# Taking the end-of-chunk decays from L itself, and moving small work off TensorE, in a Mamba-2 scan followed by an ELU feed-forward

## The chip, the cores and the metric

The kernel runs on one core of a Trainium2 chip. The metric is the device time of one execution in microseconds. Engines are called as in the profile: PE is TensorE (PEld its weight loads), DVE is VectorE, ACT is ScalarE, POOL is GpSimd, SP is the engine that issues nearly all DMAs.

## What is computed

Two stages, cut from the reference:

```python
# stage 1: x (4, 8, 768, 32), a (4, 8, 768), B and C (4, 8, 768, 16), chunk 32 there
cum = np.cumsum(log(a) of the chunk)
L = np.exp(cum[i] - cum[j]) * (i >= j)
y = (C B^T * L) x  +  (C state) * exp(cum)
state = exp(cum[last]) * state + sum_j B_j x_j exp(cum[last] - cum[j])
# stage 2: the y of all heads side by side, (3072, 256); w_in (256, 2048), w_out (2048, 256)
h = y @ w_in
g = np.where(h > 0, h, np.exp(np.minimum(h, 0)) - 1)
out = g @ w_out
```

The factor exp(cum[last] - cum[j]) is what the change is about: it is also the last column (i = last) of L.

## The kernel before, in words

**Blocks.** The 3072 tokens are cut into twelve blocks of 256 tokens, n = 0 to 11. A block is one batch entry's 256 tokens with all eight heads. The code's chunk is Q = 64 tokens, so a block has four chunks: halves u of 128 tokens, each with two chunks v. In words of the change, "block three" is n = 2 and "block four" is n = 3.

**Stage 1 of a block.** `load_bc(n)` and `load_x(n)` load B, C and x. `spread_cum(n)` loads the running sums, spread over partitions, into the tile L (partition j, then head, half u, column i). `decay_of(n, h)` turns L in place into exp(cum[i] - cum[j]) for one head, two ACT instructions of line 481, and after every fourth head POOL masks four heads in two instructions (L486). `turn(n)` transposes B and C by four PE transposes into PSUM (L389); ACT copies B to `bct` (L393) and DVE makes `ctm`, C masked by heads (L396). For n > 3 the loads come in another layout ("squares") and DVE transposes them instead: `turn_part(n, 0)` turns C, `turn_part(n, 1)` turns B (L413), `turn_part(n, 2)` makes `ctm` from SBUF (L421), `turn_part(n, 3)` makes `cts`, C times exp(cum) (L404). `first_exp(n)` makes exp(cum) spread over state rows, the tile `ec`, by a matmul with 0/1 weights `heads` (L368) and an ACT copy (L372), for n < 3; `spread_exp(n)` loads it from DRAM (`flat_exp`) for n > 2. `scaled(n)` (L379, POOL) makes `sc`, B times exp(cum[last] - cum[j]); that factor comes from the table `eb`, which `rest_of_sums` and one `turned(E, "eb", ...)` make once for n > 1. `scores(n)` are 16 small matmuls C B^T (L501, tile `g`); `weigh(n, q)` multiplies a quarter of them by L (L510, tile M); `sums(n)` are 16 small matmuls of `sc` and x (L531, tile `st`); `states(n)` chains four states S_new on DVE (L548) with a masked copy Sx on POOL (L553); `across(n)` and `inside(...)` are the matmuls that make y (L576, L595), and the copies of y to `yT` (L612).

**Stage 2.** `l1(n, i)` makes one eighth of h of block n in one PSUM bank (L627, 128x256 matmuls; with parts=2 each is cut into two of 128 columns). `elu()` takes the oldest entry of `lag`: ACT relu and exp (L640, L647), DVE combines (L649) to `g`. `l2(n, j)` multiplies `g` by two row blocks of w_out (L748). From n = 4 on a pair of blocks goes through a seven-product scheme (L699 in `front`, `mid`, `back`; L809 in `second`).

**Weights.** They arrive as 64-bit words in 16 pieces and are made into 32-bit ones on the chip: `w_take(i)` is ACT Abs (L174), a DVE low word (L183) and DVE sign (L192); `w_give(i)` is DVE L200 and L207 and then a POOL addition (L217). Pieces 8 to 15 are w_out; `l2(n, j)` needs piece 8 + j. Piece 8 is made in step 7 of the loop described next, 9 in step 9, and 10 to 15 in steps 0 to 5 of the loop of n = 2.

**Order.** The schedule is written out by hand: each engine runs its instructions in program order. After a start in which blocks 0 and 1 are brought up, a loop over twelve steps s runs the l1 of blocks 0 and 1, each step followed by pieces of block 2's stage 1. Then a loop over n = 2, 3 and i = 0 to 7 runs `l2(n - 2, i)`, `l1(n, i)`, with the stage 1 of blocks 3, 4 and 5 in `scan_ahead` and beside it; then pairs of blocks in 16 steps k each. [...] a pool of seven, `p_a`, whose buffers are given out again in the order in which they came free, and one in `p_o`.

**End.** `second(n)` sums the output of the last two blocks in the tile `c_sum`, whose parts are (block, half, column half). `store(n, at)` writes one block, 256 KB.

## Time and profile before

| | us |
|---|---|
| median of three runs (lowest, highest) | 359.23 (358.4, 359.25) |
| the profiled execution | 357.64 |
| its span in the trace | 355.9 |
| PE busy, PEld busy | 349.0, 313.4 |
| DVE, ACT, POOL busy | 242.5, 200.5, 231.8 |
| last DVE add ends | 352.5 |

The span runs from the first to the last record of the trace; the device time has 1.7 us more around it. The busy times are sums of instruction durations, so they say nothing of where in the span an engine is full; the page's 40 slices (8.9 us each) do. The profiled execution is 1.6 us below the median of the runs, so differences worked out in it are added to the median. The mean TensorE clock was 0.998 of full speed.

### The profile page before, as it was taken

To read this page: it belongs to the slowest core of one execution; us is meant where nothing else is said; L and a number is where in the kernel's file an instruction comes from. 1 tells how busy PE (TensorE), PEld (TensorE's weight loads), DVE (VectorE), ACT (ScalarE), POOL (GpSimd) and SP (SyncE) were. 2 spreads that over 40 slices of the span, in tenths; PEclk is the share of its full clock that TensorE was granted. 3 is DMA by queue.
4 is the path that set the end of the run, shared out by engine and by line. 5 is a ranking of instruction groups with operands and counts; after the bars stand their busy time and mean duration, and the time that the engine had idled before them with its cause. 6 is when DMAs were issued, how large, how long until landed. Compare 5 with 4: busy or idle time off the path is not lost.

```text
span 355.9 us, 9943 instructions
## 1 busy us (share of the span) xinstructions
PE 349.0 (98%) x3962; PEld 313.4 (88%) x3962; DVE 242.5 (68%) x500; ACT 200.5 (56%) x491; POOL 231.8 (65%) x367
## 2 busy tenths in 40 slices
PE   8899999999999999999999999999999999999995
PEld 5579888888888999899999899999899999999995
DVE  3999987993999768674677684677674555656212
ACT  4759969867425577535577535576635544444000
POOL 5553643663676997869477769477769444464973
PEclk9999999999999999999999999999999999999999
DMA  8978998470460500146500145600000100000001
GB/s 156 209 195 155 246 318 174 96 122 31 72 139 2 120 0 3 19 98 132 113 0 2 17 102 112 133 3 0 2 2 4 59 3 0 2 0 33 29 2 60
DMA packets 82742, 26.36 MB, mean 74 GB/s; under 512 B 59720, under 2 KB 78600, under 8 KB 82696
## 3 DMA queue, kind: packets, MB, share of 16 engines
q1 hardware_dynamic: 80520, 25.53, 32.2%
q8 instruction: 31, 0.51, 0.6%
q10 hardware_dynamic: 2176, 0.20, 0.5%
q14 instruction: 15, 0.12, 0.1%
HBM read 22.38 MB, written 3.34 MB: 72 GB/s over the span
## 4 chain that ended last, share of the span: by engine, by line
PE 93%; DVE 3%; ACT 1%; POOL 1%; issue 0%; POOLq 0%; DVEq 0%
PE ps_o L809 35%; PE ps_h L699 28%; PE ps_h L627 14%; PE ps_o L748 8%; PE ps_y L595 2%; PE ps_g L501 2%; PE ps_y L576 1%; PE ps_st L531 1%; PE ps_idle L232 1%; DVE mag L207 1%; DVE mag L200 1%; DVE M L510 1%; DVE sgn L192 0%; DVE g L649 0%; POOL w_in L217 0%; ACT L L471 0%
## 5 line engine op out<-in xcount | busy, mean ns | idle before, releaser
L640 ACT ACTIVATE e<-ps_h 128x512 f32<-128x512 f32 x96 | 57.0, 593 | 89.5 <-DVE ps_h L724 44.0
L809 PEld LDWEIGHTS ps_o<-w_out,g 128*128 128x128 f32 x640 | 79.9, 192 | 3.1 <-issue 0.5
L809 PE MATMUL ps_o<-w_out,g 128*128 128x128 f32 x640 | 81.0, 275 | 0.0
L649 DVE SCALAR_TENSOR_TENSOR g<-e,ps_h 128x512 f32<-128x512 f32 x96 | 65.1, 679 | 10.5 <-ACT e L647 10.4
L627 PE MATMUL ps_h<-yT,w_in 128*128 128x256 f32 (+1 forms) x272 | 60.9, 371 | 1.7 <-POOL w_in L217 1.7
L647 ACT ACTIVATE e<-e 128x512 f32<-128x512 f32 x96 | 60.9, 635 | 2.0
L776 POOL TENSOR_TENSOR g<-g 128x256 f32<-128x256 f32 x33 | 23.9, 726 | 54.4 <-DVE g L649 54.4
L627 PEld LDWEIGHTS ps_h<-yT,w_in 128*128 128x128 f32 x272 | 48.4, 190 | 9.5 <-POOL w_in L217 3.1
L809 PE MATMUL ps_o<-w_sum,g 128*128 128x128 f32 x320 | 42.9, 275 | 0.0
L809 PEld LDWEIGHTS ps_o<-w_sum,g 128*128 128x128 f32 x320 | 41.1, 192 | 1.2
L481 ACT ACTIVATE L<-L,ncum 128x64 f32<-128x64 f32 x160 | 41.0, 337 | 0.0
L699 PE MATMUL ps_h<-yT,w_in 128*128 128x256 f32 x128 | 38.8, 385 | 0.0
L732 DVE TENSOR_TENSOR ps_h<-ps_h,u_sum 128x512 f32<-128x512 f32 x32 | 22.3, 698 | 23.5 <-PE ps_h L699 23.4
L699 PE MATMUL ps_h<-y_sum,w_in 128*128 128x256 f32 x128 | 38.1, 380 | 0.0
L699 PE MATMUL ps_h<-y_sum,w_sum 128*128 128x256 f32 x128 | 38.1, 380 | 0.0
L486 POOL TENSOR_SCALAR_AFFINE_SELECT L<-L 64x512 f32<-64x512 f32 x40 | 28.8, 719 | 10.8 <-ACT L L481 9.5
L716 DVE TENSOR_TENSOR u_sum<-ps_h,u_sum 128x512 f32<-128x512 f32 x32 | 22.1, 689 | 14.5 <-ACT u_sum L709 8.1
L724 DVE TENSOR_TENSOR ps_h<-ps_h,u_sum 128x256 f32<-128x256 f32 x32 | 13.8, 432 | 26.3 <-PE ps_h L699 26.3
L748 PE MATMUL ps_o<-w_out,g 128*128 128x256 f32 x128 | 30.8, 384 | 0.0
L764 POOL TENSOR_TENSOR t<-g 128x256 f32<-128x256 f32 x40 | 28.9, 756 | 0.3
L764 POOL TENSOR_TENSOR g<-g,t 128x256 f32<-128x256 f32 x40 | 28.8, 752 | 0.3
L764 POOL TENSOR_TENSOR g<-t,g 128x256 f32<-128x256 f32 x40 | 27.9, 730 | 1.1 <-PE ps_o L809 1.1
(111 smaller groups left out, 533.9 us busy)
## 6 DMA issues: line engine op xcount, KB each, us to landing
L<-flat SPq DMA_DIRECT2D x20, 256.0 KB
w<-in_moe_w_in_dram SPq DMA_DIRECT2D x8, 512.0 KB
w<-in_moe_w_out_dram SPq DMA_DIRECT2D x8, 512.0 KB
xr<-in_x_dram SPq DMA_DIRECT2D x24, 128.0 KB
out_dram<-c_sum SPq DMA_DIRECT2D x10, 256.0 KB
bc<-in_B_dram SPq DMA_DIRECT2D x24, 64.0 KB
bc<-in_C_dram SPq DMA_DIRECT2D x22, 64.0 KB
ec<-flat_exp SPq DMA_DIRECT2D x9, 128.0 KB
```

What stands on the lines that cost most here:

```text
L481: nc.scalar.activation(L[:, h, u], L[:, h, u], ACT.Exp, bias=ncum[:, u, row:row + 1])
L486: nc.gpsimd.affine_select(out=part, in_=part, pattern=[[0, 4], [0, 2], [1, Q]], compare_op=ALU.is_ge, fill=0.0, base=0, channel_multiplier=-1)
L627: nc.tensor.matmul(out=ps[:, j, toks], lhsT=w_in[:, k, m * P:(m + 1) * P], rhs=yT[n // 2][:, k, n % 2].rearrange("p u i -> p (u i)")[:, toks],
L640: nc.scalar.activation(begun[0], lag[0][2], ACT.Relu, scale=-1.0)
L647: nc.scalar.activation(e, e, ACT.Exp, scale=-1.0)
L649: nc.vector.scalar_tensor_tensor(out=g_of[n, i], in0=e, scalar=1.0, in1=ps, op0=ALU.subtract, op1=ALU.max)
L699: nc.tensor.matmul(out=out, lhsT=lhsT, rhs=rhs, start=first, stop=True, skip_group_check=True)
L732: nc.vector.tensor_tensor(out=c2, in0=c2, in1=u[:, 0:2], op=ALU.add)
L748: nc.tensor.matmul(out=o_of[n][:, ts], lhsT=g_of[n, j][:, m % 2, ts * P:(ts + 1) * P], rhs=w_out[:, m], start=(m == 0 and ts == 0), stop=( ...
L764: nc.gpsimd.tensor_tensor(out=out, in0=in0, in1=in1, op=ALU.subtract)
L776: eng.tensor_tensor(out=b12, in0=b12, in1=b11, op=ALU.subtract)
L809: nc.tensor.matmul(out=ps[:, ts], lhsT=b[:, ts * P:(ts + 1) * P], rhs=a[:, i], start=(i == chunk[0] and ts == 0), stop=(i == chunk[-1]), s ...
```

## The change

1. **No table of decays.** `rest_of_sums`, the table `eb` (one POOL subtraction, one ACT exp, two PE transposes, one DVE copy) go. `scaled(n)` for n > 1 takes its factor from the last column of L after the masks, so it now follows all eight `decay_of`. For n = 2 it moves from step 4 to step 7; for n = 5 from i = 0 to i = 1. For n >= 6 the decays start one pair of steps earlier.
2. **exp(cum) of n = 2 by a load.** `spread_exp(2)` on SP, after `spread_cum(2)`, in place of `first_exp(2)`; the third `heads` goes.
3. **n = 3 turned by VectorE.** `load_bc(3)` brings the squares and the extra copy `b_tok`; `turn_part(3, 0..3)` at i = 0 to 3 replace `turn(3)` and `turn_exp(3)` at i = 1.
4. **Bursts joined.** `scores(2)` moves from step 7 to step 8, directly ahead of `sums(2)`; the `weigh`s of n = 2 and the y products move with it (steps 8, 9 and 11). `scores(3)` and `sums(3)` (i = 2 and i = 4) both stand at i = 3, with `states(3)`.
5. **Last store in pieces.** The last product of the last pair is made for one half of 128 tokens and then for the other, each with its own add and its own store of 64 KB; the other column half of that block is stored ahead.
6. l1(1, 2) is cut into two parts as well.

```diff
-        if n > 3:
+        if n > 2:
             st[n]["b"] = raw.tile([P, 2, NH, N], F32, tag="b", name="b_tok", bufs=2)
...
-    def rest_of_sums():
-        to_last(F[:, 0], E, nc.gpsimd)
-        nc.scalar.activation(E, E, ACT.Exp)
...
-        factor = eb0[:, :, NH * n:NH * (n + 1)] if n < 2 else eb[:, :, rows_of(n)]
+        factor = (eb0[:, :, NH * n:NH * (n + 1)] if n < 2 else
+                  s["L"][:, :, :, Q - 1].rearrange("p h u -> p u h"))
...
+                if final and half and r == 6:
+                    for ts in range(2):
+                        ps = psum([P, P], "ps_o")
+                        for i in chunk:
+                            nc.tensor.matmul(
+                                out=ps, lhsT=quarters(n, i)[3][:, ts * P:(ts + 1) * P],
+                                rhs=a[:, i], start=(i == chunk[0]), stop=(i == chunk[-1]))
+                            if i % 2:
+                                yield
+                        part = c12[:, ts]
+                        nc.vector.tensor_tensor(out=part, in0=ps, in1=part, op=ALU.add)
+                        r0 = row_of(n + 1) + ts * P
+                        nc.sync.dma_start(out=out[r0:r0 + P, 0:P], in_=part)
+                    continue
...
     spread_cum(2)
+    spread_exp(2)
...
-    eb = turned(E, "eb", 1.0, nc.vector)
...
-        l1(n, i, 2 if s < 2 else 1)
+        l1(n, i, 2 if s < 3 else 1)
         if s < 8:
             decay_of(2, s)
         if s == 7:
-            scores(2)
-            weigh(2, 0)
-            weigh(2, 1)
+            scaled(2, nc.gpsimd)
         if s % 2 == 1 and todo < 10:
             w_take(todo, nc.vector)
             w_give(todo)
...
-        if s == 4:
-            scaled(2, nc.gpsimd)
         if s == 5:
             turn(2)
-            first_exp(2)
             turn_exp(2)
         if s == 8:
             spread_cum(3)
             load_x(3)
             spread_exp(3)
-            weigh(2, 2)
-            weigh(2, 3)
             st[0] = kept
+            scores(2)
             sums(2, 0, pool=p_o, tag="o", parts=(None, last))
+            weigh(2, 0)
+            weigh(2, 1)
             states(0, last)
             st.pop(0)
             states(2)
+        if s == 9:
+            weigh(2, 2)
+            weigh(2, 3)
         if s == 10:
             spread_cum(4)
+        if s == 11:
             inside(across(2), 2)
...
-            for k in (i,) if m == 4 else (i, i + 1) if i % 2 == 0 else ():
-                if k >= 2:
-                    decay(m + k // 6, (k - 2) % 4)
+            if m > 4 and i % 2 == 0:
+                decay(m + i // 4, i % 4)
+                decay(m + i // 4, i % 4 + 1)
+            elif m == 4 and i > 1:
+                decay(m + i // 6, (i - 2) % 4)
...
-                scaled(m + 1, nc.gpsimd)
-            for k in (i,) if m == 4 else (i, i + 1) if i % 2 == 0 else ():
-                if k < 2:
-                    decay(m + 1, k + 2)
+            if m == 4 and i < 2:
+                decay(m + 1, i + 2)
+            if i == (1 if m == 4 else 0):
+                scaled(m + 1, nc.gpsimd)
...
                 if i == 1:
                     scaled(3, nc.gpsimd)
-                    turn(3)
-                    turn_exp(3)
-                if i == 2:
+                if i < 3:
+                    turn_part(3, i)
+                if i == 3:
+                    turn_part(3, 3)
                     scores(3)
+                    sums(3)
                     for q in range(4):
                         weigh(3, q)
-                if i == 4:
-                    sums(3)
                     states(3)
...
-        if k == 54:
+        if k == 53:
             store(n, 0)
+            r0 = row_of(n + 1)
+            nc.sync.dma_start(
+                out=out[r0:r0 + BLK, P:2 * P].rearrange("(t p) c -> p t c", p=P),
+                in_=c_of[n][:, 1, :, 1])
         next(steps)
     for _ in steps:
         pass
-    store(n, 1)
```

More of the change, by code (lines that the diff above doesn't have):

```diff
@@ L272 @@
     heads = [const.tile([P, NH, N], F32, name=f"heads{n}") for n in range(2)]
-    heads.append(heads[0])
     def make_heads(n):
-        cols = slice(BH + NH * n, BH + NH * (n + 1)) if n < 2 else rows_of(n)
+        cols = slice(BH + NH * n, BH + NH * (n + 1))
         nc.gpsimd.tensor_copy(
@@ L314 @@
     F = const.tile([ROWS, 2, 2, P], F32, name="F")
-    E = la
-    def rest_of_sums():
-        to_last(F[:, 0], E, nc.gpsimd)
-        nc.scalar.activation(E, E, ACT.Exp)
     flat = tc.dram_tile([2, ROWS, 2, Q], F32, name="flat")
@@ L366, in first_exp @@
         ps = psum([P, 2, P], "ps_ec")
-        rows = P if n < 2 else ROWS
         nc.tensor.matmul(
-            out=ps, lhsT=heads[n][0:rows].rearrange("p h n -> p (h n)"),
-            rhs=la0 if n < 2 else F[:, 1], start=True, stop=True)
+            out=ps, lhsT=heads[n].rearrange("p h n -> p (h n)"), rhs=la0, start=True, stop=True)
         st[n]["ec"] = att.tile([P, 2, P], F32, tag="ec", name="ec", bufs=4)
@@ L377, in scaled @@
         s["sc"] = sc = att.tile([P, 2, NH, N], F32, tag="sc", name="sc", bufs=2)
-        factor = eb0[:, :, NH * n:NH * (n + 1)] if n < 2 else eb[:, :, rows_of(n)]
+        factor = (eb0[:, :, NH * n:NH * (n + 1)] if n < 2 else
+                  s["L"][:, :, :, Q - 1].rearrange("p h u -> p u h"))
         eng.tensor_tensor(
-            out=sc, in0=s["b"] if n > 3 else s["bc"][:, 0],
+            out=sc, in0=s["b"] if n > 2 else s["bc"][:, 0],
             in1=factor.unsqueeze(3).to_broadcast([P, 2, NH, N]), op=ALU.mult)
@@ L784, with second @@
     c_of = {}
-    def second(n):
+    def second(n, final=False):
         c = c_of[n] = ffn.tile([P, 2, 2, 2, P], F32, tag="c", name="c_sum", bufs=1)
@@ L942 @@
     scaled(1, nc.gpsimd)
-    rest_of_sums()
     w_give(3)
-    make_heads(2)
     turn_exp(1)
@@ L1201 @@
     n = NP - 2
-    steps = second(n)
+    steps = second(n, True)
     for k in range(56):
```

## The prediction

> **What bounds the kernel now.** I read the engines' busy shares first, then the waits, then the timelines of 38 to 82 us and of the end.

> ```profile
> PE 349.0 (98%) x3962; PEld 313.4 (88%) x3962; DVE 242.5 (68%) x500; ACT 200.5 (56%) x491; POOL 231.8 (65%) x367
> PE   8899999999999999999999999999999999999995
> DVE  3999987993999768674677684677674555656212
> ```

> TensorE is busy in every slice but the first and the last, so each matmul removed can pay in full, if nothing else becomes late. But the mean of 68% hides VectorE: in slices 2 to 13 (9 to 116 us) it is nearly as full as TensorE. All edits but the moved exponentials from n = 6 on and the last store lie there. The waits of 57 to 80 us, and the timelines of weight loads and of VectorE, show how near it is to the limit:

> ```profile
> PEld ps_o L748 <- POOL w_out L217: 0.2, 1, 0.2
> 75.34 0.73 PEld L748 LDWEIGHTS ps_o<-w_out,g 128*128 128x128 f32 x4 [0.20 <-POOL w_out L217]
> 74.02 1.27 POOL L217 TENSOR_TENSOR w_out<-mag,w_out 128x512 uint32<-128x512 uint32 x1 [1.16 <-DVE mag L207]
> 60.24 0.43 DVE L200 TENSOR_SCALAR mag<-mag 128x512 f32<-128x512 f32 x1 [1.05 <-ACT mag L174]
> ...
> 73.18 0.69 DVE L207 SCALAR_TENSOR_TENSOR mag<-mag,sgn 128x512 uint32<-128x512 uint32 x1
> ```

> The second product l2(0, 6) needs piece 14 of the weights. VectorE finishes that piece's L207 at 73.87, GpSimd adds it until 75.29, and TensorE picks it up at 75.38, just as its own work runs out. VectorE has no idle time from 60.24 to 73.87. **So at l2(0, 6) there is no slack: work put ahead of piece 14 on VectorE delays TensorE one for one.**

> The second thing to see is what GpSimd costs VectorE. The same instruction, alone and beside GpSimd's masks (L486):

> ```profile
> 68.42 0.42 DVE L192 TENSOR_SCALAR sgn<-w 128x512 uint32<-128x512 uint32 x1
> 63.51 0.88 DVE L192 TENSOR_SCALAR sgn<-w 128x512 uint32<-128x512 uint32 x1
> 63.34 1.58 POOL L486 TENSOR_SCALAR_AFFINE_SELECT L<-L 64x512 f32<-64x512 f32 x2 [0.19 <-ACT L L481]
> 65.00 0.69 POOL L379 TENSOR_TENSOR sc<-bc,eb 128x256 f32<-128x256 f32 x1
> ```

> A whole piece (four instructions, start to the next start) takes 1.72 us alone (68.09 to 69.81) and 2.98 under the masks and `sc` (63.18 to 66.16).

> [...] L192 doubles (0.42 to 0.88), L207 (two SBUF inputs) goes from 0.69 to 1.00, while the elu of L649, which has one input in PSUM, stays at 0.68. [...] The trace has both: 0.64 us for each 128x256 on VectorE, 0.22 us for each pair of 128x128 on TensorE.

> **The change, part by part.**

> *TensorE, removed.* `first_exp(2)`: 38.97 to 39.40, 0.43 us. `turn(3)`: four transposes, 59.73 to 60.16, 0.43. The two transposes of `eb` start at 27.42, but the next product waits for yT until 27.76 anyway: 0. Joining scores and sums of n = 2 and n = 3 saves a switch of array shape each, 0.1 to 0.2 by the lead-ins (0.09 before g, 0.2 before st at 45.50): 0.25 together. l1(1, 2) in halves: eight pairs of 128-column passes of 0.1115 instead of eight of 0.216 us: +0.06. Sum -1.05 where TensorE sets the pace.

> *n = 2, a new wait.* `sums(2)` now stands directly after `scores(2)` at step 8. In the built program its `st` waits for `sc`, which needs all masks of L, and for the PSUM buffer of step 6's product, which step 6's elu frees. That elu is queued on VectorE behind all of piece 8; the two multiplications by L, which stood ahead of piece 8, now follow the elu. VectorE: `ctm` at 40.9 (41.05 before; `eb`'s 0.27 and `sc` beside piece 7's L192 are gone, but the 128 KB load of `ec` ahead of the weights in SP's queue may cost up to 0.5; I take 0.15). `ctm`, `cts` and two elus: 0.60 + 0.33 + 0.60 + 0.60, to 43.1 (the second elu waits for ScalarE's exp until 42.5). Masks and `sc` run on GpSimd from 42.9 to 45.1, so piece 8 is slowed: 1.86 us before (44.43 to 46.29), up to 2.98; I take 2.7. The elu ends at 46.5. TensorE is there at 38.97 + 3 x 1.73 + 0.09 + 0.62 = 44.9 and waits 1.6 us. `st` takes 0.59; the next l1 starts at 47.15 instead of 46.09. **+1.05 instead of -0.6.** Bounds: -0.2 (ctm 0.3 earlier, piece 8 alone) to +1.4.

> Behind `st` on TensorE stand steps 9 to 11, the y products and then l1(2, 0). ScalarE's exponentials of n = 3 and its Abs of piece 11 follow l1(2, 0), so the L200 of 60.24 moves by about +1.0.

> *n = 3, VectorE's queue.* From that L200 to piece 14's L207 there is added: the transpose of B, 0.5 (75.61 to 76.09); `ctm` from SBUF instead of PSUM, 0.98 mean and 1.39 beside GpSimd instead of 0.60: +0.6; `cts` +0.07; the four S_new, which stood behind piece 14, now ahead of it: 1.22 (74.39 to 75.61). The transpose of C falls into the idle 1.05 before the L200: 0. Masks of n = 4 now follow Sx on GpSimd and overlap less of piece 14: -0.4. Sum +2.0. So l2(0, 6) starts at 75.38 + 1.0 + 2.0 = 78.4: **+3.0**. TensorE itself would be there at about 75.8, so its savings up to here vanish in the wait. Bounds: +1.2 (n = 2 costs nothing, no contention on piece 14) to +3.8 (everything contended). From 80 us to the end TensorE is dense, so what is lost here is not regained.

> *Edits at nothing.* The decays' exponentials moved one step earlier for n >= 6, and `sc` from L's last column: ScalarE is 56% busy, GpSimd idles 54.4 us before L776, L lands long before; if a burst of 2.0 us held up an u_sum copy, up to +0.3 per pair of blocks. `sc(5)` is made later, just before its sums (about 95.4 against 95.7): 0, or +0.3. Loads of n = 3 by squares: half of the 64-byte descriptors go. `load_bc(5)` on SP now waits for `sc(3)`, some 3 us, and n = 5's C and B, L(5) and x queue behind it; they are needed some 10 us later.

> *The end.*

> ```profile
> 352.09 0.42 DVE L800 TENSOR_TENSOR c_sum<-ps_o,c_sum 128x256 f32<-128x256 f32 x1 [1.15 <-PE ps_o L809]
> 352.50:353.00 0.50, 0.00 (x0) 0.00 (x0) 0.01 (x1) 0.00 (x0) 0.00 (x0) 1.00 0.29 98
> 353.00:353.50 0.50, 0.00 (x0) 0.00 (x0) 0.00 (x0) 0.00 (x0) 0.00 (x0) 1.00 0.09 33
> 353.50:354.00 0.50, 0.00 (x0) 0.00 (x0) 0.00 (x0) 0.00 (x0) 0.00 (x0) 1.00 1.03 346
> 354.00:354.50 0.50, 0.00 (x0) 0.00 (x0) 0.00 (x0) 0.00 (x0) 0.00 (x0) 0.80 0.49 162
> ```

> The last columns are DMA share and GB/s. After the last add, 0.9 us pass before data moves, 0.75 us move 256 KB, and 1.6 us follow to 355.9. The last piece is now 64 KB (about 0.25) and its add 128x128 (0.29): -0.63. But SP issues four stores about 0.6 apart from 351.0, so the last cannot start before 352.8: I take -0.4, bounds 0 and -0.65.

> **The sum.** +3.0 - 0.4 = +2.6. The profiled execution took 357.64 (span 355.9), so 360.2 in its terms; the median of the runs is 1.59 higher, 359.23, so 361.8.

> **Rivals.**
> - *VectorE keeps up and TensorE's savings count: faster.* Then -1.05 - 0.4 gives 357.7. For it: all removed matmuls lie on a dense TensorE. It decides if piece 14 is added by the time TensorE arrives (about 74.4 then): VectorE's chain would have to be 4 us shorter than I have it, which means no `st` wait and no contention for any piece from 11 to 14, which costs some 2.7 us now (0.4 + 1.1 + 1.2), and more. Against it: VectorE's queue is longer by instructions that can be counted. Chance 0.2, as the overlaps with GpSimd are the least certain term.
> - *The two waits are half as long.* Without contention on the pieces +3.0 becomes about +0.3, and with the end 359.1, no change. Chance 0.1.
> - *Slower still.* Full contention, +3.8, and a late ScalarE burst in each of three pairs, +0.3 each, at an end that gains nothing: 363.9. Inside the slower case, 0.15 of it.

> **Numbers.** Slower 0.7, faster 0.2, same 0.1; 0.3%, 1.1 us, is about what a measurement of this kernel can tell from no change. The slower case alone spans 360.4 to 363.4; the range reaches down to 357.8 to take in the same case and part of the faster one.

> **What would show it.** Right: a wait of PE or PEld at `st` of n = 2, before step 9, released by L642 or L372; one of 2 us or more at l2(0, 6) on GpSimd's w_out; M of n = 2 after piece 8; the same spacing of products from 85 us on; some 3.0 us from the last add to the end instead of 3.4. Wrong: l2(0, 6) before 76.5, piece 8 near 1.9 us, or a new wait in the loops over n >= 4.

## The result, and the profile after

| | before | after | ratio (95% interval) |
|---|---|---|---|
| first comparison, medians | 358.81 | 363.85 | 1.0138 (1.0103 to 1.0173) |
| the same two kernels in a later group of runs | 358.14 | 366.43 | 1.0229 (1.0202 to 1.0255) |

The change made the kernel slower by 5.0 us, in the second set by 8.3. The forecast was slower, 361.8 us with a range up to 363.4, so the direction was right and the size was short. The profiled execution after took 363.84 us, its span is 362.1 (355.9 before), and its mean TensorE clock 0.995 (0.998 before, where all that is missing lies behind 354 us, when the last product is over).

In the new kernel's line numbers l1 is L620, g L494, st L524, M L503, S_new L541, the elu L642, the masks L479, `sc` L372, y L569 and L588, l2 L741; the lines of the weights are as before.

The sliced rows of the page, for PE, DVE and the granted clock (answering to the two rows of before):

```profile
PE   8899879889999999999999999999999999999996
DVE  3988985995599867676578585577675556556212
PEclk9999989999999999999999999999999999999999
```

TensorE, full in slices 5, 6, 8 and 9 before (counted from one, some 9 us each), has holes there now: two places, n = 2 and n = 3. And slice 6 of the clock row is not full. TensorE's timeline of the first place, after and then before:

```profile
43.52 0.69 PE L494 MATMUL ps_g<-ctm,bct 32*64 32x128 f32 x32
47.26 0.90 PE L524 MATMUL ps_st<-xr,sc 64*32 64x64 f32 x40 [3.04 <-issue]
48.09 6.53 PE L620 MATMUL ps_h<-yT,w_in 128*128 128x256 f32 x24
...
55.77 1.99 PE L741 MATMUL ps_o<-w_out,g 128*128 128x256 f32 x8
```

```profile
45.50 0.66 PE L531 MATMUL ps_st<-xr,sc 64*32 64x64 f32 x40
52.82 1.89 PE L748 MATMUL ps_o<-w_out,g 128*128 128x256 f32 x8
```

`st` waits 3.04 us (1.6 forecast), and what follows is slow as well: 24 products take 6.5 us instead of 24 x 0.216 = 5.2. Stretches of the same timeline (stretch, its length, PE busy and products, granted clock, DMA share, GB/s) say why:

```profile
43.49:46.90 3.41, 0.73 (x33) 1.00 0.75 248
46.90:50.31 3.41, 3.05 (x45) 0.50 0.97 345
50.31:53.72 3.41, 3.41 (x17) 1.00 1.12 290
```

For 3.41 us TensorE ran at half its clock ("half clock" below). That term stands nowhere in the prediction. The trace names no engine that ended the wait of `st` ("issue"). The VectorE rows and the two GpSimd rows beside them show what it was waiting for:

```profile
43.40 0.85 DVE L183 TENSOR_SCALAR w_out<-w 128x512 f32<-128x512 uint32 x1
44.17 0.89 DVE L192 TENSOR_SCALAR sgn<-w 128x512 uint32<-128x512 uint32 x1
44.98 0.85 DVE L200 TENSOR_SCALAR mag<-mag 128x512 f32<-128x512 f32 x1
45.87 0.69 DVE L207 SCALAR_TENSOR_TENSOR mag<-mag,sgn 128x512 uint32<-128x512 uint32 x1
46.48 0.68 DVE L642 SCALAR_TENSOR_TENSOR g<-e,ps_h 128x512 f32<-128x512 f32 x1
43.31 1.47 POOL L479 TENSOR_SCALAR_AFFINE_SELECT L<-L 64x512 f32<-64x512 f32 x2 [0.82 <-ACT L L474]
44.86 0.69 POOL L372 TENSOR_TENSOR sc<-bc,L 128x256 f32<-128x256 f32 x1
```

Piece 8 lies from its first to its third instruction under the masks and `sc`: 3.08 us from start to the elu behind it, 1.86 before:

```profile
44.43 0.55 DVE L183 TENSOR_SCALAR w_out<-w 128x512 f32<-128x512 uint32 x1
46.29 0.68 DVE L649 SCALAR_TENSOR_TENSOR g<-e,ps_h 128x512 f32<-128x512 f32 x1
```

The elu ends at 47.16, and `st` starts 0.1 later; `sc` had been there since 45.55. That it was the elu, and not a load, is shown below, by piece 8 made one step later.

The second place, TensorE and then VectorE and GpSimd up to piece 14:

```profile
71.73 0.70 PE L494 MATMUL ps_g<-ctm,bct 32*64 32x128 f32 x32 [1.24 <-DVE ctm L414]
82.11 1.99 PE L741 MATMUL ps_o<-w_out,g 128*128 128x256 f32 x8 [2.14 <-POOL w_out L217]
63.80 0.43 DVE L200 TENSOR_SCALAR mag<-mag 128x512 f32<-128x512 f32 x1 [0.61 <-ACT mag L174]
73.83 1.11 DVE L397 TENSOR_TENSOR cts<-bct,ec 128x256 f32<-128x256 f32 x1
76.20 1.29 DVE L541 SCALAR_TENSOR_TENSOR S_new<-S_new,ec,ps_st 128x64 f32<-128x64 f32 x4
78.23 0.89 DVE L192 TENSOR_SCALAR sgn<-w 128x512 uint32<-128x512 uint32 x1
79.95 0.69 DVE L207 SCALAR_TENSOR_TENSOR mag<-mag,sgn 128x512 uint32<-128x512 uint32 x1
77.82 1.81 POOL L479 TENSOR_SCALAR_AFFINE_SELECT L<-L 64x512 f32<-64x512 f32 x2
```

l2(0, 6) starts at 82.11: 6.73 later than before, 3.7 later than forecast. From the L200 of piece 11 to the end of piece 14's L207 VectorE takes 16.8 us (13.6 before). After 90 us the spacing is that of before but for 0.3 us between 117 and 168. The end: the last add is over at 359.43, the span ends 2.7 later (3.4 before). So the span's +6.2 is 6.7 at l2(0, 6), 0.3 after it, and about -0.8 at the end.

### The profile page after: what moved, and what is told of

Same layout as the page of the kernel before. It is cut to its first block, busy times and chain, and to the rows that moved or that the text cites. A ratio compares the mean times of both kernels' runs of the same rounds, so it can differ in the third digit from the quotient of the medians.

```text
span 362.1 us, 9943 instructions
## 1 busy us (share of the span) xinstructions
PE 349.5 (97%) x3962; PEld 313.8 (87%) x3962; DVE 242.6 (67%) x502; ACT 199.8 (55%) x488; POOL 231.7 (64%) x365
## 4 chain that ended last, share of the span: by engine, by line
PE 83%; DVE 6%; DMA 3%; POOL 2%; SPq 2%; issue 2%; ACT 2%; POOLq 0%; DVEq 0%; ACTq 0%
PE ps_o L816 34%; PE ps_h L692 27%; PE ps_h L620 8%; PE ps_o L741 6%; PE ps_y L588 2%; PE ps_g L494 2%; SPq L129 2%; DMA b_tok<-in_B_dram 1%; PE ps_st L524 1%; DMA w<-in_moe_w_in_dram 1%; PE ps_y L569 1%; PE ps_idle L232 1%; DVE mag L207 1%; POOL w_in L217 1%; DVE mag L200 1%
## 5 line engine op out<-in xcount | busy, mean ns | idle before, releaser
L816 PEld LDWEIGHTS ps_o<-w_out,g 128*128 128x128 f32 x640 | 79.9, 192 | 3.1 <-issue 0.5
L642 DVE SCALAR_TENSOR_TENSOR g<-e,ps_h 128x512 f32<-128x512 f32 x96 | 65.0, 679 | 15.2 <-ACT e L640 15.0
L620 PE MATMUL ps_h<-yT,w_in 128*128 128x256 f32 (+1 forms) x280 | 61.5, 369 | 1.6 <-POOL w_in L217 1.5
L620 PEld LDWEIGHTS ps_h<-yT,w_in 128*128 128x128 f32 x280 | 49.6, 193 | 9.3 <-POOL w_in L217 2.9
L769 POOL TENSOR_TENSOR g<-g 128x256 f32<-128x256 f32 x33 | 24.5, 745 | 50.4 <-DVE g L642 50.3
L816 PE MATMUL ps_o<-w_sum,g 128*128 128x128 f32 x304 | 40.9, 275 | 0.0
L816 PEld LDWEIGHTS ps_o<-w_sum,g 128*128 128x128 f32 x304 | 39.2, 192 | 1.2
L479 POOL TENSOR_SCALAR_AFFINE_SELECT L<-L 64x512 f32<-64x512 f32 x40 | 28.2, 704 | 12.6 <-ACT L L474 9.0
L741 PE MATMUL ps_o<-w_out,g 128*128 128x256 f32 x128 | 31.0, 385 | 2.5 <-POOL w_out L217 2.5
L741 PEld LDWEIGHTS ps_o<-w_out,g 128*128 128x128 f32 x128 | 23.7, 190 | 6.7 <-POOL w_out L217 3.3
```

Of the source, the lines that this page charges most:

```text
L479: nc.gpsimd.affine_select(out=part, in_=part, pattern=[[0, 4], [0, 2], [1, Q]], compare_op=ALU.is_ge, fill=0.0, base=0, channel_multiplier=-1)
L620: nc.tensor.matmul(out=ps[:, j, toks], lhsT=w_in[:, k, m * P:(m + 1) * P], rhs=yT[n // 2][:, k, n % 2].rearrange("p u i -> p (u i)")[:, toks],
L642: nc.vector.scalar_tensor_tensor(out=g_of[n, i], in0=e, scalar=1.0, in1=ps, op0=ALU.subtract, op1=ALU.max)
L741: nc.tensor.matmul(out=o_of[n][:, ts], lhsT=g_of[n, j][:, m % 2, ts * P:(ts + 1) * P], rhs=w_out[:, m], start=(m == 0 and ts == 0), stop=( ...
L769: eng.tensor_tensor(out=b12, in0=b12, in1=b11, op=ALU.subtract)
L816: nc.tensor.matmul(out=ps[:, ts], lhsT=b[:, ts * P:(ts + 1) * P], rhs=a[:, i], start=(i == chunk[0] and ts == 0), stop=(i == chunk[-1]), s ...
```

## The experiments

Theory A: the order on VectorE makes two long waits, and a wait of 2 to 3 us costs clock on top. Rivals: the loads (data late through SP's queue), the added work itself, another cause of the slow products. In every entry "before" is the kernel before on the same chip (357.87, 357.95, 358.14 and 358.26 in the four groups); an entry gives the median and, in brackets, the ratio to that and its 95% interval.

One caution for what follows. Two profiled executions can stand apart before any edit acts. The kernel before, and the same kernel with nothing but its end edited (the last store in pieces, below):

```profile
15.27 0.60 PE L441 MATMUL ps_x<-low,ident 128*128 128x256 bf16 x4
27.76 10.93 PE L627 MATMUL ps_h<-yT,w_in 128*128 128x128 f32 x64
14.63 0.60 PE L441 MATMUL ps_x<-low,ident 128*128 128x256 bf16 x4
27.12 10.93 PE L627 MATMUL ps_h<-yT,w_in 128*128 128x128 f32 x64
```

The second is 0.65 us ahead here, and still at 269 us. Over the sixteen profiles these four products of L441 (L434 in the new kernel; "the mark" below) start between 14.63 and 15.78. So differences under 1 us between two executions are read from the mark, not from the start of the span. For the changed kernel's profile it makes 0.1.

**The changed kernel again.**

> The changed kernel unchanged, on the same chip as the others, for a sharper time of it and for the spread of its granted clock. Theory A (the clock halves for windows of 3.4 us whose place against the program differs from run to run): times spread over 1.5 us or more, 362.0 to 364.5, with the mean clock 0.990 to 1.000 going along; Theory B (the half clock belongs to the program): the mean clock is 0.995 in every run and the spread no more than that of the kernel before, 1 us.

Six runs from 363.99 to 367.34. A window of 3.41 us at half clock lowers the mean over 362 us by 0.0047, so the mean clock gives their number (the traces of the two profiled runs, 363.84 and 367.21, show one and two):

| mean clock | windows | times |
|---|---|---|
| 0.994 and 0.995 (first set) | 1 | 362.52 to 364.29, four runs |
| 0.994 | 1 | 363.99, one run |
| 0.991 | 2 | 365.99 to 367.21, four runs |
| 0.986 | 3 | 367.34, one run |

Time and windows go together, as in theory A, though the times lie above its range (up to 364.5), and at least one window in each of ten runs was more than I had expected. The windows are only a part of the difference between the two comparisons. The profiled execution here (367.21, two windows) is 3.4 us longer than the first one (363.84, one window). The second window, behind l2(0, 6), accounts for 1.7. Another 1.7 was lost ahead of l1(1, 0), which starts 13.49 behind the mark instead of 11.83: in the start ScalarE waited 2.02 for a load of weights, and in the first profile not at all.

```profile
20.27 0.69 ACT L174 ACTIVATE mag<-w 128x512 f32<-128x512 f32 x1 [2.02 <-DMA w<-in_moe_w_in_dram]
18.47 0.68 ACT L174 ACTIVATE mag<-w 128x512 f32<-128x512 f32 x1
```

Whether the other runs of this group share that late load, the record does not show.

**Filling the wait, first try.**

```diff
-        for at, n in enumerate(ns):
+        for at, n in enumerate(ns * 5 if ns == (2,) else ns):
+            at = 0 if ns == (2,) else at
```

> Theory A (the long wait of TensorE at st of n = 2 also costs clock): in the changed kernel TensorE stands still from 44.2 to 47.26 us and then runs 47 to 50.3 us at a granted clock of 0.50. Here the 32 products of scores(2) are issued five times (same result, 2.5 us more work on TensorE), which fills that wait. st still starts at about 47.2, as the elu that it waits for is not touched, but the clock stays 1.00, st takes 0.6 us instead of 0.9 and the next l1 steps run at full speed: l2(0, 0) at about 54.4 instead of 55.77, the whole 1.3 to 1.5 us faster than the changed kernel (about 362.4 against 363.85). Theory B (the slow products of 47 to 50 us have another reason, contention in SBUF or waits for M): same times as the changed kernel, 363.9, or up to 2.5 us slower, since work was added.

368.18 (1.0274, 1.0244 to 1.0304): slower by 4.3 than the changed kernel in its first comparison. The half clock did not come at 47 us, but a new stop did, in the middle of `st`:

```profile
46.93 0.32 PE L525 MATMUL ps_st<-xr,sc 64*32 64x64 f32 x9 [0.45 <-issue]
49.99 0.54 PE L525 MATMUL ps_st<-xr,sc 64*32 64x64 f32 x31 [2.74 <-issue]
q8 instruction: 1, 0.02, 1.9%
```

The last row is from the DMA view of 46.9 to 50.0 us: the instruction queue moved one packet. 128 products and their weight loads are 256 instructions; I take it that TensorE had run out of them (a "stop for instructions" below: TensorE idle, with no semaphore that ends it). That idle time brought a half clock of its own at 51.25 (TensorE busy for 1.26 of the 3.41 us ahead of it). The try was confounded by its own size.

**Filling it with few, long products.**

```diff
         gs = [psum([P, len(ns), 2, 2, Q], "ps_g") for _ in range(4)]
+        if ns == (2,):
+            for q in range(12):
+                nc.tensor.matmul(
+                    out=gs[q % 4].rearrange("p n u v q -> p (n u v q)"), lhsT=ident,
+                    rhs=ident.unsqueeze(1).to_broadcast([P, 2, P]), start=True, stop=True)
```

> The wait of TensorE at st of n = 2 is filled again, but by twelve products of 128x256 ahead of scores(2) (results overwritten; 2.6 us more work on TensorE in 24 instructions) instead of 128 small ones, which were 256 instructions and ran into a stop of 2.74 us at whose middle the instruction queue moved a packet. Theory A (a stretch of TensorE mostly idle halves the clock for the 3.4 us that follow): st at about 47.2, no half clock from 47 to 50 us, no new stop; l2(0, 0) at 54.3 to 54.6 (55.77 in the changed kernel) and, where no other wait trips the clock, the whole about 362.4. Theory B (the slow stretch is not from the idle time): l2(0, 0) at 55.8 and 363.9 as in the changed kernel. Theory C (any work added to TensorE costs its own time): about 366.

367.20 (1.0261, 1.0241 to 1.0282), mean clock 1.000 in all four runs. I had mis-sized the filler: the twelve products of 128x256 are 24 instructions of 0.216 us in the trace, 5.2 us together, and `st` started at 49.54. Even so l2(0, 0) came only 1.0 us later than in the changed kernel, because from `st` to l2(0, 0) it took 7.22 us instead of 8.51. Of the other 2.0 us, most is two more stops for instructions far away, 0.48 at 227 us and 1.37 at 280 us, the latter with no other transfer running:

```profile
281.58 0.59 PE L697 MATMUL ps_h<-yT,w_in 128*128 128x256 f32 x2 [1.37 <-issue]
q8 instruction: 1, 0.02, 2.2%
```

It stands behind 192 small products of y. As I read it, the added instructions had moved the next packet into that burst.

**The same with four products, and the number of instructions kept** (l1(1, 2) whole again).

```diff
-        l1(n, i, 2 if s < 3 else 1)
+        l1(n, i, 2 if s < 2 else 1)
...
+            for q in range(4):
```

> The wait of TensorE at st of n = 2 filled with four products of 128x256 ahead of scores(2), 8 instructions of 0.216 us each and their weight loads (about 1.75 us of added work; results overwritten), and l1(1, 2) whole instead of in halves, so that the number of TensorE's instructions stays the same and the packets of its instruction queue fall at the same places. Theory A (the half clock of 46.9 to 50.3 us follows from a stretch of 3.4 us in which TensorE worked for only 0.7): st still at about 47.2, clock 1.00, the step from st to l2(0, 0) 7.2 us instead of 8.51; l2(0, 0) at about 54.5, l2(0, 6) at about 80.8; total -1.3 (362.5). Theory B (the slow stretch has another cause): 8.5 us from st to l2(0, 0), total unchanged.

```profile
46.92 0.65 PE L529 MATMUL ps_st<-xr,sc 64*32 64x64 f32 x40 [0.71 <-issue]
54.11 1.99 PE L746 MATMUL ps_o<-w_out,g 128*128 128x256 f32 x8
78.36:81.77 3.41, 1.37 (x6) 1.00 1.16 163
81.77:85.18 3.41, 3.41 (x9) 0.50 0.01 1
```

From `st` to l2(0, 0) 7.19 us, as theory A has it: work added to TensorE made this stretch 1.3 us shorter, and the stop at 280 us is not there. But the total is 364.07 (1.0173, 1.0149 to 1.0198), no gain: now the wait at l2(0, 6) fell into one window (1.37 us busy of 3.41), and the clock behind it was half. The penalty had moved.

**n = 2 with the bursts apart** (`scores(2)`, M and y where they were; all else of the change stays).

```diff
+            scores(2)
+            weigh(2, 0)
+            weigh(2, 1)
...
-            scores(2)
             sums(2, 0, pool=p_o, tag="o", parts=(None, last))
```

> Undoes of the joined bursts only those of n = 2: scores(2), its M and y stand again where they stood before; sc(2) from L and the loaded ec stay. Theory A (step 6's elu behind piece 8 sets the start of st, and the join brings that wait): st now waits only for sc, to about 45.6; no half clock; l2(0, 0) at 52.8 to 53.0 (55.77 in the changed kernel), l2(0, 6) at about 79, as VectorE's queue of n = 3 stays; total -3.0 to -3.4, about 360.6. Theory B (the load of ec ahead of the others in SP's queue makes the data late): st not before 47, total within 0.5 of the changed kernel.

The mechanism was as expected: `st` at 45.95, no half clock there. The total was not: 363.57 (1.0148, 1.0124 to 1.0171). y of n = 2 stopped 0.74 us about where the first filler had stopped, behind some 1,450 products and weight loads of TensorE. Ahead of that g had waited 0.70 for `ctm`: ScalarE had waited 1.36 for the load of piece 6 (0.36 before), and all behind it came late. So l2(0, 0) came at 54.55. Two of the four runs had one window at half clock, in the profiled one behind the wait of 2.23 us at l2(0, 6). The other two, at full clock, took 362.15 and 363.36: most of the loss is there without any half clock.

**n = 3 as before.**

```diff
-        if n > 2:
+        if n > 3:
             st[n]["b"] = raw.tile([P, 2, NH, N], F32, tag="b", name="b_tok", bufs=2)
...
-                if i < 3:
-                    turn_part(3, i)
-                if i == 3:
-                    turn_part(3, 3)
+                    turn(3)
+                    turn_exp(3)
+                if i == 2:
                     scores(3)
-                    sums(3)
...
+                if i == 4:
+                    sums(3)
                     states(3)
```

> Undoes of the change all that concerns n = 3: its B and C by the old layout, the four transposes on TensorE, scores at i = 2, sums and states at i = 4. Theory A (VectorE's longer queue between the L200 of piece 11 and the L207 of piece 14 costs 3.2 us, 16.8 against 13.6): L200 of piece 11 stays at about 63.8, the L207 of piece 14 ends at about 77.5, l2(0, 6) at about 79.0 instead of 82.11; total -3.0 to -3.2, about 360.7; no wait for ctm ahead of g of n = 3. Theory B (piece 14 is late because the weights arrive late or because of the loads in SP's queue): l2(0, 6) still after 81.

362.08 (1.0120, 1.0090 to 1.0150). The wait at l2(0, 6) is gone, and from l2(0, 0) to l2(0, 6) it takes 23.1 us instead of 26.3: -3.2, theory A. In the profiled run, with no half clock at all, l2(0, 6) starts at 77.60. `st` waited 3.04 there too, but across two windows (2.08 and 1.69 us busy of 3.41), and from `st` to l2(0, 0) it took 7.18 instead of 8.51. The other five runs have mean clocks of 0.985 to 0.995: the wait at `st` stays, and with it, presumably, its penalty.

**Both undone** (the last two diffs together).

> The bursts of n = 2 apart and n = 3 as before: what stays of the change is sc from L, no table, the loaded ec of n = 2, l1(1, 2) in halves, the decays moved for n >= 6 and the last store in pieces. Theory A (the two edits undone are all that costs): l2(0, 6) at about the 75.4 of the kernel before, 0.85 won at the end, 357.0 to 357.4 against 357.9 of before. Theory B (sc from L makes st of n = 2 wait until 45.9 and the y products of n = 2 then stop for instructions, as they did for 0.74 us with the bursts apart): l2(0, 0) at 54.5 instead of 52.82, l2(0, 6) at about 76.5 to 77, the whole 358.5 to 359.0.

358.45 (1.0023, 1.0012 to 1.0033), near theory B: nearly all of the loss lies in the two places, and what is left of the change costs 0.4 to 1.2 us instead of winning. y of n = 2 stopped 0.29 us for instructions. Read from the mark, l1(1, 0) started 0.67 earlier than before, and l2(0, 0) and l2(0, 6) 0.37 later.

**Piece 8 one step later**, behind `states(2)`; the join stays.

```diff
-        if s % 2 == 1 and todo < 10:
+        if s in (1, 3, 5, 9):
             w_take(todo, nc.vector)
...
             states(2)
+            w_take(todo, nc.vector)
+            w_give(todo)
+            w_load(todo + 6)
+            todo += 1
```

> The join of n = 2 stays, but piece 8 of the weights is made one step later, behind states(2), so that step 6's elu, M and S_new stand ahead of it on VectorE. Theory A: the wait at st ends with sc at about 45.6 instead of 47.26 (1.3 us of wait instead of 3.0), the clock stays at 1.00; l2(0, 0) at about 52.5 to 53.0; if pieces 8 and 9 back to back do not delay the elus of steps 7 and 8, total about 360.6 (-3.2). Theory B (sc or a load sets st): st stays at 47 and the total at 363.9.

```profile
44.71 0.66 PE L524 MATMUL ps_st<-xr,sc 64*32 64x64 f32 x40 [0.94 <-POOL sc L372]
52.22 0.76 PE L569 MATMUL ps_y<-cts,Sx 32*64 32x64 f32 x8 [1.21 <-DVE M L503]
```

With the elu ahead of piece 8, `st` starts as soon as `sc` is there. So the elu had set it, not the loads. The clock stayed at 1.00 in three of the six runs. But pieces 8 and 9 now stand in one row ahead of M, and y waits for that: 363.10 (1.0162, 1.0134 to 1.0190).

**states(3) behind piece 14.**

```diff
                     for q in range(4):
                         weigh(3, q)
+                if i == 4:
                     states(3)
```

> The changed kernel with one line moved: states(3), the four S_new on VectorE, at i = 4 behind piece 14 instead of at i = 3 ahead of it. Theory A (at l2(0, 6) VectorE's queue is paid one for one): the L207 of piece 14 ends 1.2 us earlier (79.4 instead of 80.6), the wait of TensorE at l2(0, 6) falls from 2.14 to about 0.9, l2(0, 6) at 80.9 instead of 82.11; the y products of n = 3 do not wait, as S_new still ends before 83; total -1.2, and more where the shorter wait no longer trips the clock. Theory B (GpSimd's masks, not VectorE's count of instructions, set piece 14): they then fall fully on piece 14, which takes 3.0 instead of 2.7, and the gain is 0.3 to 0.9.

The wait of 2.14 us at l2(0, 6) is gone:

```profile
82.08 1.99 PE L741 MATMUL ps_o<-w_out,g 128*128 128x256 f32 x8
47.18:50.59 3.41, 2.68 (x44) 0.50 1.04 381
50.59:54.00 3.41, 3.41 (x9) 0.50 1.11 308
```

From the L200 of piece 11 to the end of piece 14's L207 it is 14.7 us instead of 16.8. That is 2.2, not 1.2: with Sx out of the way GpSimd's masks (L479, 76.75 to 78.33) are over before piece 14 begins at 78.81, which then takes 1.71 us instead of 2.67. The total hardly shows it, 362.90 (1.0139, 1.0119 to 1.0158): the two further rows show that this time the clock was half for two windows behind the wait at `st`.

**The two orders together**, piece 8 behind all M and states of n = 2, and states(3) later; and the same with n = 3 as before.

```diff
             states(2)
+            weigh(2, 2)
+            weigh(2, 3)
+            w_take(todo, nc.vector)
+            w_give(todo)
...
-        if s == 9:
-            weigh(2, 2)
-            weigh(2, 3)
...
+                if i == 4:
                     states(3)
```

> The changed kernel with two orders changed and no work: piece 8 behind all four M and the states of n = 2 at step 8 instead of at step 7, and states(3) at i = 4 behind piece 14. Theory A (the two long waits and the half clocks that follow from them are the loss): st of n = 2 at about 44.7 behind sc, y of n = 2 at 50.7 without a wait for M, l2(0, 0) at about 52.3, from there to l2(0, 6) 24.2 us as with the later states, so 76.4 (75.4 in the kernel before); clock 0.998 to 1.000 in nearly all runs; the whole 358.4 to 358.8 against 358.0. Theory B (the extra loads, the transposes on VectorE and the squares of n = 3 cost by themselves): 360 or more.

> As the kernel with the orders changed, but n = 3 turned on TensorE with its bursts as in the kernel before. Theory A: l2(0, 0) at about 52.3 (52.82 before), l2(0, 6) at 74.8 to 75.4, where piece 14 sets it as before, the last store in pieces -0.4: 357.0 to 357.6 against 358.0. Theory B (what was dropped, the table above all, still costs elsewhere): 358.4 as with both parts undone.

361.01 (1.0076, 1.0057 to 1.0095) and 361.25 (1.0088, 1.0070 to 1.0107). The first number is theory B's, but its reason is only a part; the second is neither's. `st` starts right behind `sc`, but now y waits:

```profile
53.30 0.45 PE L569 MATMUL ps_y<-cts,Sx 32*64 32x64 f32 x20 [2.00 <-DVE g L642]
```

Part of y needs a PSUM buffer that an elu frees, and on VectorE that elu now stands behind pieces 8 and 9 (it starts at 52.56). In both profiled runs the clock was half behind that wait (1.46 and 1.41 us busy of 3.41); three runs of the first kernel at full clock still took 360.2 to 360.6. With the half clock taken off (l2(0, 0) and the l1 behind it 1.7 and 1.5 us longer than usual), from l2(0, 0) to l2(0, 6) it takes 23.7 with n = 3 on VectorE and 22.7 with n = 3 on TensorE (22.56 before). So turning n = 3 on VectorE costs about 1.0 us even in the better order, and 3.2 in the changed kernel (26.3 against 23.1 with n = 3 as before). The second profile also has a half clock in the start, at 14.8 us, behind a wait of 2.23 for the first copy of y (1.41 us busy of 3.41), ahead of anything that the change edits.

**Parts alone, on the kernel before.** The last store in pieces (the diff's part of `second` and of the last loop, nothing else):

> The kernel before with the last store in pieces as the one edit. Theory A: it is worth what the two profiles show from the last product on, the span -0.85 (2.67 us instead of 3.4 from the last add, and an add of 0.29 instead of 0.42): 357.0 against 357.9. Theory B (SP's issues, four stores about 0.6 apart, hold the last one): -0.4 or less, 357.5.

357.57 (0.9988, 0.9977 to 0.9999), -0.4 us. The -0.8 of the changed kernel's profile is not repeated: in this profile 3.5 us pass from the last add to the end. The profiles fall into two sets. With this edit and n = 3 in squares, 2.7 us pass in all nine; with this edit and n = 3 as before, 3.3 to 3.6 in all six (3.4 in the kernel before). In these six and in the kernel before, an instruction queue moved a packet in the last 2.6 us, in the nine it did not:

```profile
q14 instruction: 1, 0.01, 0.6%
```

So what the edit wins seems to hang on where such a packet falls; no run changed that alone.

With `rest_of_sums` moved behind two elus as well:

```diff
     scaled(1, nc.gpsimd)
-    rest_of_sums()
...
     weigh(1, 1)
     elu()
+    rest_of_sums()
     states(1)
```

> The kernel before with the last store in pieces, and with rest_of_sums (GpSimd's subtraction and ScalarE's exponential of the table) moved behind the two elus of block 1 that it stood ahead of. Theory A (in the kernel before, that exponential, at 21.08 us behind a wait of 0.48 for GpSimd, held up ScalarE's relu and exp and with them the y products of block 1; this and not the two transposes is what dropping the table saved): l1(1, 0) at about 27.0 instead of 27.76, kept through to the end as far as piece 14 allows it: the whole -0.7 - 0.4, 356.9 against 357.9. Theory B (the 0.75 us is eaten at l2(0, 6), where VectorE's pieces decide): 357.5, as with the last store alone.

357.57 again (0.9983, 0.9967 to 1.0000). Read from the mark, l1(1, 0) started 0.67 earlier (11.82 instead of 12.49), as much as in the changed kernel, so it is `rest_of_sums` that this was about and not the two transposes, which are still there. But l2(0, 0) came 0.37 later than with the store alone, and so did l2(0, 6). Theory B, but for the place: the gain is lost before 53 us, not at l2(0, 6). ScalarE, early now, waited for the load of piece 6 of the weights:

```profile
34.66 0.69 ACT L174 ACTIVATE mag<-w 128x512 f32<-128x512 f32 x1 [0.85 <-DMA w<-in_moe_w_in_dram]
```

With the store alone it did not wait for a load there. From there to 44 us ScalarE has no idle time, and the l1 behind g waited 0.40 for an elu.

**Sums one step later**, on the kernel with both parts undone:

```diff
+        if s == 9:
+            st[0] = kept
+            sums(2, 0, pool=p_o, tag="o", parts=(None, last))
+            states(0, last)
+            st.pop(0)
+            states(2)
         if s % 2 == 1 and todo < 10:
...
-            st[0] = kept
-            sums(2, 0, pool=p_o, tag="o", parts=(None, last))
-            states(0, last)
-            st.pop(0)
-            states(2)
         if s == 10:
             spread_cum(4)
+        if s == 11:
             inside(across(2), 2)
```

> As the kernel with both undone, but sums(2) and states(2) one l1 step later (step 9, ahead of piece 9) and the y products at step 11, so that TensorE does not wait for sc [...]. Theory A (with no wait at st, y and n = 3, the products removed from TensorE pay): st at about 46.2 without a wait, l2(0, 0) at about 51.7 (52.82 before), l2(0, 6) at about 74.4, end -0.85: 355.8 to 356.4 against 357.9 of before. Theory B (VectorE's pieces 8 to 14 set the pace anyway, so TensorE only arrives earlier at a wait): l2(0, 6) at 75.3 with a wait of 1 us, 357.0.

358.91 (1.0026, 1.0016 to 1.0037), a miss on both theories: y waited 0.84 us for an elu behind piece 9 on VectorE. No version that keeps more of the change than the store beats the kernel before. The store, alone or with the moved exponential, is the best that was run, and its interval alone just leaves out no change.

## Why the prediction was right or wrong

The direction and the two places were right, and the sum was too small. The step that failed first is "n = 2, a new wait", +1.05: it measured +2.95, because piece 8 took longer than I took, and because the half clock behind the wait had no term at all. The second is "n = 3, VectorE's queue", +2.0: it measured +3.2, and ScalarE added 0.5 that I had not counted. That the number came as near as it did is in part luck: my base of 359.23 was the median of three runs, and the later groups gave 357.9 to 358.3. And the upper end of my range, 363.4, left out my own rival of 363.9.

**TensorE, removed (-1.05).** The products went, and TensorE did come earlier: l1(1, 0) 0.66 earlier, read from the mark. I had priced the table at 0, counting its two transposes and missing GpSimd's subtraction and ScalarE's exponential, which held up the relu and exp behind them. In the sum it changed nothing: the gain ended in the wait at `st`, and alone it was lost before l2(0, 0).

**n = 2, a new wait (+1.05).** The mechanism was right, its size was wrong, and a term was missing; l2(0, 0) moved by 2.95.
- The wait was 3.04, not 1.6. TensorE was there at 44.2 instead of 44.9 (the exponential again, which lengthens the wait but delays nothing), and the elu ended at 47.16 instead of 46.5. Piece 8 took 3.08 where I took 2.7 and had 2.98 as the end of the bound, and it began at 43.4, not 43.1.
- The missing term: the half clock, 1.3 us up to l2(0, 0) by the filled wait (8.51 against 7.19), and by the same wait of 3.04 without a half clock (7.18, n = 3 as before). The bound "+1.4" for n = 2 left it out, so the upper end of the range was too low from this step on.

**ScalarE's Abs of piece 11 and L200 (+1.0).** They stand behind l1(2, 0), as argued, and that moved by 3.05 (54.55 to 57.60). L200 moved by 3.56: before, ScalarE reached the elu of l1(2, 0) just as that product ended; now it is busy without a pause from the copies of y (55.48) on, and comes to it 0.5 later. With n = 3 as before it is the same.

**n = 3, VectorE's queue (+2.0).** Measured +3.2. `ctm` from SBUF (1.29 instead of 0.60) and S_new (1.21) were right. The transposes were as priced (0.64 us for 128x256 on VectorE, 0.48 to the next start; a pair of 128x128 on TensorE took 0.22). `cts` was not +0.07 but +0.7: it ran beside GpSimd's addition of piece 13 (1.11 us instead of 0.41). The -0.4 for less contention was not there: piece 14 took 2.67 instead of 2.89, but piece 12 took 3.31 instead of 2.98. That VectorE is slower beside GpSimd the rows show (L192 took 0.41 in piece 13 and 0.92 beside the masks in piece 12); why, no run shows. With S_new ahead of piece 14 the masks still lie on it; the later states took them off (1.0 us). A wait of 1.24 at g for `ctm` was not foreseen; it came on top for TensorE but is inside VectorE's chain, so it does not add.

**The end (-0.4).** Right for that edit alone, 357.57 against 357.95, within an interval of 0.0 to 0.8; in the changed kernel's profile it was -0.8. That it lay between is luck, as I did not know of the packet that goes with the difference.

**Edits at nothing.** SP's queue and the load of `ec` did not set `st`, as its start straight behind `sc` shows. That loads decide nothing is too much to say: up to step 8 ScalarE waits for weights in most profiles, 0.4 us before, 2.0 with the bursts apart, and 0.9 with the moved exponential, which has no load of `ec`. No run took out that load alone, so its share is open; my "up to 0.5" for it was an estimate. A +0.2 at 137.8 us appears in every version with the moved decays and not in the store alone; that is inside the "+0.3 per pair" given, seen once. What was not priced at all: the stops for instructions. In the versions with the bursts apart they took 0.3 to 0.7 us at y. One reading was loose: of slices 2 to 13 slice 10 shows VectorE at 30%; the sum does not use it.

**The rivals.** "VectorE keeps up" was wrong as argued. "Slower still" came nearest, 363.9, but by luck: the contention in it was there, the late ScalarE bursts were worth 0.3 in all and not 0.9, the end did gain, and it had no half clock.

**The sum** in the profiled execution's terms: +3.0 - 0.4 forecast, and found +6.73 at l2(0, 6) (2.95 up to l2(0, 0), 3.78 from there), +0.3 later, -0.8 at the end in this profile and -0.4 with that edit alone.

**Left open.** No order was found in which the change costs nothing; each wait removed brought out the next, so whether there is one stays open. Why y of n = 2 loses 0.4 us in the versions with the bursts apart besides its stop was not followed up.

## What to carry to other kernels

A wait of TensorE is not priced by its length alone: add up how busy TensorE is over any 3.4 us around it, and if no more than 43% of that is work, the most that had a half clock behind it here, expect another 1.3 to 1.7 us in a part of the runs. Joining small bursts moves the buffers they free (`st` waited 3.04 us for one here), and four of the five stops for instructions (0.29 to 2.74 us) lay in such bursts or right behind one; ask for each burst which instruction of a busy engine frees its PSUM buffer, and what stands in the queue ahead of that. When one wait is taken away and the total does not move, look for the next wait and for the clock, before giving up the reason.

## What the runs showed of the hardware that was not expected

```profile
51.35:54.76 3.41, 1.46 (x85) 1.00 1.07 159
54.76:58.17 3.41, 3.41 (x9) 0.50 0.76 222
```

in the kernel with the two orders, while none inside the program with 1.69 us or more at full clock was (the least is 45.58 to 48.99 with n = 3 as before). So a wait of 2.0 us can be enough, and one of 3.04 us can pass if it lies across two windows, as it did there. Where between 43 and 50% the line lies, no window inside the program shows.

**TensorE stopped in bursts of small products with no semaphore to end the stop.** Stops of 0.29, 0.74, 1.37 and 2.74 us stood in such bursts or right behind one, each with one packet of the instruction queue in it or up to 1.0 us ahead of it (0.9 to 1.1 us long). The queue, q8, moved 31 such packets of 16 KB in the kernel before, which has 7,924 products and weight loads (256 to a packet), and 32 in the first filler, which has 256 instructions more, so I take it for TensorE's. With the stop of 0.48 at 227 us it is five stops, and in all five TensorE went on 2.2 to 2.5 us after the start of the packet. Those of the first filler and of the bursts apart fell at the same place in the instructions (about the 1,445th product or weight load), and the one at 280 us came and went with the number of instructions 230 us earlier. The link is read from these coincidences; no run changed the packets alone.
